# Eight of ten spectral blocks by seven half products of Strassen, transposed, with sixteen row scans moved behind them

## The chip, the cores and the metric

One Trainium2 chip, one core of it. The metric is the time in device microseconds of one execution of the whole kernel. The core has engines that run beside each other, each in the order of its own instructions: TensorE (PE in the profile, with PEld for its loads of weights), VectorE (DVE), ScalarE (ACT), GpSimd (POOL) and SyncE (SP), which here only issues transfers. An instruction that waits for a semaphore holds everything behind it on its engine. PSUM holds the results of matmuls, SBUF everything else on the core; DRAM is reached by DMA.

## What is computed

Everything is fp32; S = 2048 rows, D = 512 columns, 32 heads of 16.

```python
def reference(x, wqkv, wo, ..., dft_seq_re, dft_seq_im, dft_hid_re, dft_hid_im, gate_w):
    g = sigmoid((x * gate_w).sum(-1, keepdims=True))
    q, k, v = heads(x @ wqkv)                           # 32 heads of 16
    o = softmax(q @ k.T / 4) @ v                        # per head, 2048 x 2048 scores
    a = o @ wo
    re, im = x @ dft_hid_re.T, x @ dft_hid_im.T         # 2048 x 512
    y = dft_seq_re @ re - dft_seq_im @ im               # 2048 x 2048 by 2048 x 512, twice
    return g * a + (1 - g) * y
```

The part of the change is the second product of y, dft_seq_im times im. A "spectral block" t is 128 rows of it (128 x 2048 by 2048 x 512); there are sixteen.

## The kernel before, in words

**Numbers.** A product of two fp32 operands is made of three products of rounded parts: hi·hi, hi·lo, lo·hi, where hi is the operand rounded and lo is the rest. Each of them is issued as two matmuls of 64 rows (`halves_of`, L181), which run together into two PSUM banks. So a block of 128 x 128 times 128 x 512 is six matmuls, and a spectral block, with sixteen of these, 96.

**Front (to about 672 us).** The projections to q, k and v, re and im (im is kept negated, `b`; both are stored to DRAM in 128-row tiles, `ab_d`), the whole product with dft_seq_re, and the first six blocks with dft_seq_im. Beside these products run "scans". A scan (n of 0..1023, 64 for each of the 16 pairs of heads) gives the maximum of 512 scores for 128 rows, for two heads; the softmax needs the maxima of its pair before that pair's turn. `FRONT` = 724 scans are made in the front (660 of them folded: two matmuls L154, an ACT pass L158 for every other one, a DVE pass L160). How densely they stand beside the products is set by the spacings `PACE`, `SUMS`, `BESIDE`, `PART` and `SWAP`.

**Rear.** One loop over 512 "steps" (L1010): a pair p has 32 steps, step = 32p + i, with sixteen blocks of 128 keys for each half h of the queries. In a step the scores of one block of keys go to PSUM (`qk_both`, L234: one exp of 1024 columns; `qk_single`, L242: two of 512), and the exps of an earlier step are multiplied by the values (`pv`, L755). Beside that, a step has one more piece of work:

- steps 2 to 300: one scan (`next_scan`, L998: two matmuls L135, a DVE reduce L137), number n = 723 + step;
- from `MIX` = 301 on: one slot of `outputs()` (L961). First the ten spectral blocks t = 6..15, sixteen slots of six matmuls each (L907), to step 460; then, from `OUT` = 461, the product of the heads' outputs with wo (`mix_heads` for t = 0..15, then `mix_some`).

Scans and slots share one pair of PSUM banks (`pair_banks`, L743). On an odd step the order is scores, scores, slot; on an even one slot, scores, scores and two blocks of values' products.

**Buffers for the rows.** A pair's q and k rows (eight transfers, `row_loads`, L89 to L100, together 1.57 MB) live in two tiles of the pool `stk`, which has six: three pairs' worth. Who takes them: `load_use(p + 1)` at i = 18 of each pair, for the exps of the next pair (L1014; it also loads ones, L116, and the maxima `m_d`, L118); `load_scan`, for the next pair to be scanned, when n % 64 = 54 (L1002), ten scans before its first use; later `load_y` (L865), for y of four blocks at a time. The pair that is in use holds two tiles for its 32 steps, the pair that is scanned holds two for its 64 scans.

**Spectral operands.** For a spectral block the quarter blocks of dft_seq_im come from DRAM (`load_unit`, L883, tile `craw`, two buffers) and are split into hi and lo on DVE (L890, L891); im stays in SBUF in 32 tiles `b0` to `b31` (hi and lo). At the end of a block two DVE operations (L911) add it, times 1 − g, to the y of the front, which comes from and goes back to DRAM (`y_d`, L898 and L912). `load_y` fetches the sums at steps 436 (t = 0..7) and 480 (t = 8..15).

**Order of transfers.** All transfers named here are issued by SP, in the order of the program, and at most eight of them are under way: each waits for the end of the one eight places before it. The heads' outputs are written by POOL's queue (L774 `r_d`, L783 `o_d`). Near the end SP issues, in this order: the rows of the heads' outputs (`output_rows`, L847), then `output_last(1)` (L862), whose eight loads wait for the store `o_d` of the last pair but one, then the stores of the result (L945). `take_in` (L872) is the DVE operation that adds a finished product with wo, times g, to y.

Of the kernel before, what the change touches and what calls it, by code (L numbers as in the profile page):

```python
# [10 lines left out]
F32 = mybir.dt.float32  # L11
# [7 lines left out]
P = 128  # L19
# [27 lines left out]
MIX = TOTAL - FRONT + 1  # L47
OUT = MIX + NB * LATER
SLOW = 3
SCANS_IN = 0  # L50
AHEAD = (30, 31, 37, 44)


def build(tc, xT, wqkv, wo, wrT, wiT, cr, ci, gate, out):
    nc = tc.nc
    with ExitStack() as ctx:
# [12 lines left out]
        m_d = [dram.tile([2, 4, 2, NB, 32], F32, name=f"m_d{p}") for p in range(NP)]  # L69
        ab_d = [[dram.tile([P, D], F32, name=f"ab_d{i}_{t}") for t in range(NB)] for i in range(2)]  # L70
        y_d = [dram.tile([P, 4, D], F32, name=f"y_d{c}") for c in range(NC)]
# [115 lines left out]
        def block(i):  # L187
            return big.tile([P, 512], F32R, tag=f"b{i}", name=f"b{i}")
# [541 lines left out]
        with ExitStack() as pa:  # L730
# [12 lines left out]
            def pair_banks():  # L743
                return wide(SCANS_IN, "s1")
# [58 lines left out]
            def output_operands():  # L803

                for n in range(2 * ND - 2):
                    b = [block(6 + 2 * n + i) for i in range(2)]
                    raw = (ap.tile([P, D], F32, tag="craw", name="wor", bufs=2) if n == ND - 2 else
                           ap.tile([P, D], F32, tag="take", name="wor", bufs=3))
# [65 lines left out]

            raws, units = [], [(t, u) for t in range(NB - LATER, NB) for u in range(NU)]
            parts = []

            def load_unit():
                if units:
                    t, u = units.pop(0)  # L880
                    raw = ap.tile([P, D], F32, tag="craw", name="craw", bufs=2)
                    raws.append(raw.rearrange("p (c q) -> p c q", q=P))
                    nc.sync.dma_start(raws[-1], ci[t, :, u * CS:(u + 1) * CS, :])  # L883
# [30 lines left out]

            def take_in_beside(t, ps, add):

                o = ap.tile([P, D], F32, tag="take", name="take", bufs=2)
                nc.scalar.mul(o, ps, g[:, t:t + 1])
                add.tensor_add(ys[t], ys[t], o)

# [40 lines left out]
            def outputs():  # L961

                for t in range(NB - LATER, NB):
                    yield from spectral(t)
                for c in range(NC):
                    for t in range(4 * c, 4 * c + 4):
                        yield from mix_heads(t, (2, 2, 2, 3) if t < 2 * SLOW and t % 2 == 0 else (4, 5))
                    if c < 2:
                        output_rows(c + 2)
                for t in (8, 9, 10):  # L970
                    yield from mix_some(t, (0, 1))
                for t in range(3):
                    yield from mix_some(t, (0, 1))
                yield
# [35 lines left out]
            for step in range(NP * PERIODS):  # L1010
# [42 lines left out]
                if halved and halved[0][0] <= step:  # L1053
# [82 lines left out]
```

## Time and profile before

| | |
|---|---|
| time, median of 3 runs | 1726.67 us (1726.31 to 1727.58) |
| time of the profiled execution | 1727.06 us |
| its span in the profile | 1725.1 us |
| instructions | 36058 |
| bytes moved by DMA | 195.53 MB |
| L234, the exps of 1024 columns | 512 x 1131 ns |
| `craw<-ci` transfers | 64 of 256 KB |

The profile is that of one execution. Its page gives busy time for each engine (matmuls overlap, so PE's sum can be near the span while more work would fit), then the span in slices, the queues, a chain of what ended last, and groups of instructions. A group's line has its place in the code, engine, operation, output and inputs, the shape, the count, then busy time and mean, then the idle time ahead of it and what ended that. The view by windows gives, for a stretch of the span, each engine's busy time with its count of instructions, then TensorE's granted clock, the DMA engines' busy share and the GB/s moved. The timeline gives start, duration, engine, line, output and input; for SP an entry is the issue of a transfer, not its landing.

### The profile page before, as it was taken

The numbers are of one execution on the slowest core, as the hardware profiler recorded it, in microseconds if no ns is written. First come the engines' busy times: TensorE is split into PE (matmuls) and PEld (weight loads), VectorE is DVE, ScalarE is ACT, GpSimd is POOL, SyncE is SP. The second block draws the span as 40 slices with busy tenths as digits, with TensorE's granted clock in tenths as the row PEclk, the third lists the DMA queues.
The fourth block names the chain that finished last, engine by engine and source line by source line (L and its number), as shares of the span: only waits on it lengthen the run. The fifth ranks groups of instructions, "written<-read, shape, count | busy, mean of one in ns | idle before, by whom it ended". The sixth has DMA issues, their size and how long they took to land.

```text
span 1725.1 us, 36058 instructions
## 1 busy us (share of the span) xinstructions
PE 1711.2 (99%) x13656; PEld 1039.2 (60%) x13656; DVE 1089.1 (63%) x2060; ACT 1507.0 (87%) x2489; POOL 653.0 (38%) x774
## 2 busy tenths in 40 slices
PE   9999999999999999999999999999999999999998
PEld 6888888989888885333333333333455555555554
DVE  5898888999999996666666666666512222122333
ACT  6447889888888888999999999999988888888876
POOL 3672435655555762223223242322322322223222
PEclk9999999999999999999999999999999999999999
DMA  7783457533337763143323332251333254254723
GB/s 255 239 288 76 150 159 214 160 112 114 103 110 209 157 134 74 31 78 58 66 59 66 55 80 47 57 104 41 61 84 93 68 116 90 67 144 141 184 66 126
DMA packets 126750, 195.53 MB, mean 113 GB/s; under 512 B 56192, under 2 KB 58736, under 8 KB 119664
## 3 DMA queue, kind: packets, MB, share of 16 engines
q1 hardware_dynamic: 85392, 171.64, 37.4%
q0 software_dynamic: 40608, 20.54, 5.7%
q8 instruction: 107, 1.75, 0.4%
q10 hardware_dynamic: 576, 1.05, 0.2%
q14 instruction: 67, 0.55, 0.1%
HBM read 130.55 MB, written 63.18 MB: 112 GB/s over the span
## 4 chain that ended last, share of the span: by engine, by line
PE 95%; DMA 1%; DVE 1%; issue 1%; ACT 1%; POOL 0%; SPq 0%; DVEq 0%; POOLq 0%; ACTq 0%
PE pvb L755 28%; PE xy L185 25%; PE s L210 18%; PE s L154 10%; PE s L185 9%; PE s L135 5%; DMA q_d<-eh 0%; DMA raws<-wqkv 0%; DVE fold L160 0%; DMA b<-o_d 0%; PE s L554 0%; DVE y L872 0%; ACT fold L158 0%; DVE s L278 0%; DVE mx L137 0%
## 5 line engine op out<-in xcount | busy, mean ns | idle before, releaser
L234 ACT ACTIVATE eb<-s 128x1024 f32<-128x1024 f32 x512 | 578.9, 1131 | 64.5 <-PE s L210 64.4
L242 ACT ACTIVATE e<-s 128x512 f32<-128x512 f32 x1022 | 608.5, 707 | 0.4 <-PE s L210 0.4
L137 DVE TENSOR_REDUCE mx<-s 128x2 f32<-128x1024 f32 x364 | 441.3, 1224 | 188.6 <-PE s L135 188.2
L755 PE MATMUL pvb<-eb,va 128*17 128x512 f32 x2052 | 513.0, 597 | 0.0
L755 PE MATMUL pvb<-e,va 128*17 128x512 f32 x2044 | 512.1, 597 | 0.0
L160 DVE CUSTOM_DVE_ANT_0 fold<-s,fold 128x512 f32<-128x512 f32 x660 | 444.0, 690 | 52.5 <-PE s L154 24.3
L158 ACT ACTIVATE fold<-s 128x512 f32<-128x512 f32 x660 | 390.4, 604 | 72.8 <-PE s L154 50.5
L210 PEld LDWEIGHTS s<-qs,ks 50*128 50x128 f32 x2048 | 214.9, 184 | 355.4 <-ACT eb L234 254.9
L210 PE MATMUL s<-qs,ks 50*128 50x512 f32 x2048 | 420.4, 434 | 0.0
L185 PE MATMUL xy<-b,c 64*128 64x512 f32 x2448 | 396.9, 392 | 0.3 <-ACT c L333 0.3
L154 PE MATMUL s<-ks,qs 48*128 48x512 f32 x1320 | 314.4, 405 | 1.7 <-DVE mx L160 1.0
L185 PEld LDWEIGHTS xy<-b,c 64*128 64x128 f32 x2448 | 283.3, 187 | 17.0 <-issue 1.0
L154 PEld LDWEIGHTS s<-ks,qs 48*128 48x128 f32 x1320 | 172.7, 184 | 46.9 <-DVE mx L160 12.7
L774 POOL DMA_DIRECT2D r_d<-lc x31 | 18.2, 586 | 458.3 <-DVE lc L773 458.3
L755 PEld LDWEIGHTS pvb<-eb,va 128*17 128x17 f32 x2052 | 70.5, 96 | 189.8 <-issue 182.6
L135 PE MATMUL s<-ks,qs 48*128 48x512 f32 x728 | 151.7, 394 | 1.1 <-DVE mx L137 0.7
L767 POOL DMA_DIRECT2D lc<-ob x124 | 63.0, 515 | 155.0 <-DVE ob L764 154.7
L185 PE MATMUL xy<-w,b 64*128 64x512 f32 x768 | 115.2, 392 | 0.0
L365 POOL TENSOR_TENSOR c<-craw,c 128x512 fp32r<-128x512 f32 x84 | 109.6, 1304 | 6.7
L185 PE MATMUL s<-b,chi 64*128 64x512 f32 x654 | 103.0, 391 | 0.0
L364 POOL CAST c<-craw 128x512 fp32r<-128x512 f32 x84 | 53.4, 636 | 124.9 <-PE xy L185 119.9
L890 DVE CAST chi<-craw 128x512 fp32r<-128x512 f32 x40 | 19.7, 493 | 111.7 <-PE s L185 83.2
(133 smaller groups left out, 1532.2 us busy)
## 6 DMA issues: line engine op xcount, KB each, us to landing
qs<-q_d SPq DMA_DIRECT2D x66, 256.0 KB
craw<-ci SPq DMA_DIRECT2D x64, 256.0 KB
craw<-cr SPq DMA_DIRECT2D x60, 256.0 KB
ks<-k_d SPq DMA_DIRECT2D x44, 256.0 KB
qs<-q_d SPq DMA_DIRECT2D x66, 128.0 KB
ab_d<-ab SPq DMA_DIRECT2D x32, 256.0 KB
y_d<-y SPq DMA_DIRECT2D x32, 256.0 KB
o_d<-oh POOLq DMA_DIRECT2D x30, 256.0 KB, 13.3
```

The source lines that it names most:

```text
L135: nc.tensor.matmul(ps[:, j, :], qs[b:b + 48, qb * P:(qb + 1) * P], ks[b:b + 48, c * 512:(c + 1) * 512], start=True, stop=True)
L137: nc.vector.tensor_reduce(mx[p][:, :, qb, c], ps, axis=AX.X, op=ALU.max)
L154: nc.tensor.matmul(ps, qs[b:b + 48, qb * P:(qb + 1) * P], ks[b:b + 48, c * 512:(c + 1) * 512], start=True, stop=True)
L158: nc.scalar.activation(fold[j], ps, AF.Relu)
L160: nc.vector.tensor_tensor_reduce(out=fold[j], in0=ps, in1=fold[j], scale=1.0, scalar=-3.0e38, op0=ALU.add, op1=ALU.max, accum_out=mx[p][:, ...
L185: nc.tensor.matmul(ps[j], lhs[r], rhs[r], start=first, stop=last)
L210: nc.tensor.matmul(pss[j], ks[b:b + 50, kb * P:(kb + 1) * P], qs[b:b + 50, q0:q0 + 512], start=True, stop=True)
L234: nc.scalar.activation(e, ps, AF.Exp, scale=SCALE)
L242: nc.scalar.activation(e[j], pss[j], AF.Exp, scale=SCALE)
L365: sub(lo, raw, hi.bitcast(F32))
L755: nc.tensor.matmul(pvb[r:r + VC, :], va[:, kb, 2 * p + j, :], es[c][j], start=kb == 0, stop=kb == NB - 1, tile_position=(0, r))
L767: nc.gpsimd.dma_start(lc[32 * n:32 * n + 32, :], ob[r + DH:r + VC, :].rearrange("p (s e) -> p s e", e=16))
```

## The change

`FRONT` goes from 724 to 708: sixteen scans move from the front to the rear, whose `MIX` goes from 301 to 317 (`PART` from 2.07 to 2.15, so that the scans left are spread over the same products). Of the ten spectral blocks of the rear only t = 6 and 7 stay as they were (steps 317 to 348). The other eight, t = 8..15, are computed as one transposed product: 512 x 2048 (im transposed) by 2048 x 1024. It is cut into quadrants, 256 x 1024 by 1024 x 512, and in place of their eight products Strassen's seven are made (`CROSSES`: sums and differences of quadrants on the left and on the right), each in two halves f of 128 columns of im and eight slots: 112 slots of six matmuls in place of 128, steps 349 (`HALVED`) to 460. `OUT` stays 461.

For these products:

- twelve operands a product (`form_unit`): sums or differences of one or two 256 KB pieces, which `begin_unit` loads three steps ahead (the right operand from a new input `ct`, the left one from the stored im, in pieces of 128 columns); on DVE an addition or subtraction where there are two pieces, then a copy (hi) and a subtraction (lo). The tile `craw` has eight buffers in place of two;
- at the end of each half (`gather`) DVE copies one PSUM bank and adds the other, POOL adds it into the results that need it, and when a quadrant is done DVE transposes it in 32 x 32 squares (three steps later) and SP stores it to DRAM in four transfers (five to eleven steps later);
- at steps 482 to 489 the eight transposed blocks are loaded one by one (`load_turned`, tile with three buffers), and three steps later each is added to y on DVE (`take_turned`).

`output_rows(0)` moves from step 449 to 453. `load_y` for t = 8..15 stays at step 480. `take_in_beside`, which nothing calls, goes.

The core of the diff:

```diff
-FRONT = 564 + 16 * LATER
+CROSS = 8
+SAVED = 2 * CROSS
+FRONT = 564 + 16 * LATER - SAVED
-PACE, SUMS, BESIDE, PART, SWAP = 3.9, 5.2, 2.72, 2.07, 2.97
+PACE, SUMS, BESIDE, PART, SWAP = 3.9, 5.2, 2.72, 2.15, 2.97
 MIX = TOTAL - FRONT + 1
-OUT = MIX + NB * LATER
+OUT = MIX + NB * LATER - SAVED
+HALVED = MIX + NB * (LATER - CROSS)
+TURNED = 482
+CROSSES = [([((0, 0), 1), ((0, 1), 1)], [((1, 1), 1)]),
...
+            for n, (left, right) in enumerate(CROSSES):
+                crossed += [(NB * n + at, n, left if f is not None else right, f, u)
+                            for at, f, u in ((-8, 0, 0), (-6, None, 0), (-5, None, 1), (-4, None, 2), (-2, 0, 1),
+                                             (-1, None, 3), (0, None, 4), (2, None, 5), (3, None, 6), (4, None, 7),
+                                             (6, 1, 0), (7, 1, 1))]
+            def begin_unit(at, n, terms, f, u):
...
+                for (a, b), sign in terms:
+                    raw = ap.tile([P, 512], F32, tag="craw", name="craw", bufs=8)
+                    if f is None:
+                        nc.sync.dma_start(raw, ct[8 * a + u, :, 512 * b:512 * b + 512])
+                    else:
+                        e = 256 * a + P * f
+                        nc.sync.dma_start(raw.rearrange("p (s e) -> p s e", e=P),
+                                          b_d[2 * b + u][:, :, e:e + P].rearrange("s p e -> p s e"))
...
+            def form_unit(at, n, terms, f, u):
...
+                if len(raws) > 1:
+                    (nc.vector.tensor_add if terms[1][1] > 0 else nc.vector.tensor_sub)(raws[0], *raws)
...
+                nc.vector.tensor_copy(hi, raws[0])
+                nc.vector.tensor_sub(lo, raws[0], hi.bitcast(F32))
+            def finish(r, quadrant, f, x):
...
+                def square():
+                    turn.append(cw.tile([P, 512], F32, tag=("chi", "clo")[f], name="turn"))
+                    nc.vector.transpose(turn[0], x)
+                def store(a):
+                    e = 256 * k + P * f + 32 * a
+                    nc.sync.dma_start(yt_d[j].rearrange("(b i) e -> i b e", i=32)[:, :, e:e + 32],
+                                      turn[0][32 * a:32 * a + 32, :].rearrange("p (b e) -> p b e", e=32))
+                finishing.append((r + 3, square))
+                for a in range(4):
+                    finishing.append((r + 5 + 2 * a, lambda a=a: store(a)))
+            def gather(n, f, ps, r):
+                t = place(28 + f if n == 0 else 30 + f if n == 1 else None)
+                nc.vector.tensor_copy(t, ps[:, 0, :])
+                nc.vector.tensor_add(t, ps[:, 1, :], t)
...
+            def crosses():
+                for n in range(len(CROSSES)):
+                    for f in range(2):
+                        ps = pair_banks()
+                        for u in range(8):
+                            left, right = sets[f, u // CS], sets[None, u]
+                            q = slice((u % CS) * P, (u % CS + 1) * P)
+                            for i, (a, b) in enumerate(((0, 0), (0, 1), (1, 0))):
+                                halves_of((ps[:, 0, :], ps[:, 1, :]), left[a][:, q], right[b],
+                                          u == 0 and i == 0, u == 7 and i == 2)
+                            if u < 7:
+                                yield
+                        gather(n, f, ps, now[0] - HALVED)
+                        yield
+            def load_turned(t):
+                y = ap.tile([P, D], F32, tag="take", name="turned", bufs=3)
+                nc.sync.dma_start(y, yt_d[t // 4 - 2][(t % 4) * P:(t % 4 + 1) * P, :])
+                turned_[t] = y
+            def take_turned(t):
+                nc.vector.scalar_tensor_tensor(ys[t], turned_.pop(t), gm[:, t:t + 1], ys[t], op0=ALU.mult, op1=ALU.add)
...
-                for t in range(NB - LATER, NB):
+                for t in range(NB - LATER, NB - CROSS):
                     yield from spectral(t)
+                yield from crosses()
...
-                if step in (OUT - 12, OUT + 1):
+                if step in (OUT - 8, OUT + 1):
                     output_rows(int(step > OUT))
-                if step in (OUT - 25, (NP - 1) * PERIODS):
+                if step in (OUT - 25, TURNED - 2):
...
                 pend.append((p, h, kb, es))
+                crossing(step - HALVED)
+                if TURNED <= step < TURNED + CROSS:
+                    load_turned(NB - CROSS + step - TURNED)
+                if TURNED + 3 <= step < TURNED + 3 + CROSS:
+                    take_turned(NB - CROSS + step - TURNED - 3)
```

More of the change, by code (lines that the diff above doesn't have):

```diff
@@ L69, in build @@
         m_d = [dram.tile([2, 4, 2, NB, 32], F32, name=f"m_d{p}") for p in range(NP)]
-        ab_d = [[dram.tile([P, D], F32, name=f"ab_d{i}_{t}") for t in range(NB)] for i in range(2)]
+        b_d = [dram.tile([4, P, D], F32, name=f"b_d{n}") for n in range(NB // 4)]
+        ab_d = [[dram.tile([P, D], F32, name=f"ab_d_{t}") for t in range(NB)],
+                [b_d[t // 4][t % 4] for t in range(NB)]]
+        yt_d = [dram.tile([D, D], F32, name=f"yt_d{j}") for j in range(2)]
         y_d = [dram.tile([P, 4, D], F32, name=f"y_d{c}") for c in range(NC)]
@@ L913, in spectral @@
                 yield
[L915 to L919, printed above, removed]
+            crossed, begun, sets = [], {}, {}
+            for n, (left, right) in enumerate(CROSSES):
[3 more added lines that the diff above has]
+                                             (6, 1, 0), (7, 1, 1))]
@@ new lines, in form_unit @@
+            def form_unit(at, n, terms, f, u):
+                raws = begun.pop(at)
+                if len(raws) > 1:
+                    (nc.vector.tensor_add if terms[1][1] > 0 else nc.vector.tensor_sub)(raws[0], *raws)
+                base = 6 + 2 * u if f is None else 22 * f + 2 * u
+                hi, lo = block(base), block(base + 1)
+                nc.vector.tensor_copy(hi, raws[0])
+                nc.vector.tensor_sub(lo, raws[0], hi.bitcast(F32))
+                sets[f, u] = hi, lo
@@ new lines, in crossing, with place @@
+            def crossing(r):
+                for job in crossed:
+                    if job[0] == r + 3:
+                        begin_unit(*job)
+                for job in crossed:
+                    if job[0] == r:
+                        form_unit(*job)
+                for job in finishing[:]:
+                    if job[0] == r:
+                        finishing.remove(job)
+                        job[1]()
+            finishing, places, tiles = [], [0], {}
+            def place(i=None):
+                if i is None:
+                    i = (4, 5, 26, 27)[places[0] % 4]
+                    places[0] += 1
+                return block(i).bitcast(F32)
```

39 lines of the change are left out of this document (35 added, 4 removed), and 6 rows, old and new, of the table CROSSES.

## The prediction

> **What bounds the kernel now.** First the page: who is busy, and what the chain that ended last runs through.
>
> ```profile
> span 1725.1 us, 36058 instructions
> PE 1711.2 (99%) x13656; PEld 1039.2 (60%) x13656; DVE 1089.1 (63%) x2060; ACT 1507.0 (87%) x2489; POOL 653.0 (38%) x774
> PE 95%; DMA 1%; DVE 1%; issue 1%; ACT 1%; POOL 0%; SPq 0%; DVEq 0%; POOLq 0%; ACTq 0%
> ```
>
> TensorE's chain is the span. Which engine sets its pace differs by stage, so next the view by windows (busy time and count of PE, PEld, DVE, ACT, POOL; granted clock; DMA share; GB/s), for the front, the scan stage, the spectral stage and the stage of outputs:
>
> ```profile
> 400.00:425.00 25.00, 25.00 (x213) 22.58 (x213) 23.22 (x71) 22.06 (x40) 14.17 (x15) 1.00 0.35 101
> 700.00:1200.00 500.00, 500.00 (x3696) 191.42 (x3692) 338.79 (x312) 500.00 (x792) 151.02 (x227) 1.00 0.33 64
> 1238.00:1586.70 348.70, 348.70 (x2873) 184.86 (x2873) 71.44 (x126) 311.06 (x480) 95.69 (x143) 1.00 0.40 99
> 1588.00:1690.00 102.00, 102.00 (x830) 54.19 (x828) 34.12 (x51) 84.39 (x128) 28.38 (x43) 1.00 0.50 128
> ```
>
> The front is TensorE's: 25 us for 213 matmuls, 0.117 each. In the rear a step has three exps, so a step takes 500/264 = 1.894 us in the scan stage, where ACT is busy throughout, and 348.7/160 = 2.179 in the spectral stage, where ACT rests and TensorE sets the pace. No wait of TensorE is long anywhere: whatever the change makes TensorE wait for comes on top.
>
> **The change part by part.**
>
> *Work taken away.* Sixteen folded scans of two matmuls leave the front: 16 x 2 x 0.117 = 3.8 us. In the rear the number of steps stays, sixteen of them become scan steps in place of spectral ones: 16 x (2.179 - 1.894) = 4.6 us. The half products have the slots and matmuls of the blocks that they replace. Gain 8.4 us, where nothing is late.
>
> *Rows for the scans (the largest term).* `load_scan` is asked for when n % 64 = 54. That was step 35 + 64k and is now 51 + 64k, for pairs 12 to 15. Look at SyncE's timeline and waits:
>
> ```profile
> 672.75 0.58 SPq L100 DMA_DIRECT2D ks<-k_d  x1
> 676.64 0.56 SPq L100 DMA_DIRECT2D qs<-q_d  x1
> 725.23 0.56 SPq L100 DMA_DIRECT2D ks<-k_d  x1
> 730.84 0.60 SPq L100 DMA_DIRECT2D qs<-q_d  x1
> 757.19 0.56 SPq L100 DMA_DIRECT2D ks<-k_d  x1
> ...
> SPq L100 <- PE s L210: 224.0, 13, 46.1
> ```
>
> 725.23 is `load_scan(12)`: it waited for L210, the last use of pair 0 at step 31, and took its two tiles. 757.19 is `load_use(2)` at step 50; it took the tiles of pair 11, scanned until step 44. With the change step 50 comes first and takes pair 0's tiles; at step 51 the six tiles belong to the pair in use, the next one, and pair 11, whose last scan is now step 60. The built program says so: the first load of pair 12's rows waits for pair 11's last scan matmul, and pairs 13, 14 and 15 likewise. The scan of step 61 needs these rows. TensorE takes its instructions in order, so behind that scan stand step 61's other scores, the values' products and everything after. ACT then runs dry. Four times TensorE waits for eight loads, less one step.
>
> How long eight loads take is in the windows over two bursts of before:
>
> ```profile
> 672.00:674.00 2.00, 2.00 (x18) 0.67 (x14) 1.28 (x2) 1.95 (x4) 0.78 (x2) 1.00 0.35 131
> 674.00:676.00 2.00, 2.00 (x20) 0.72 (x22) 1.34 (x2) 2.00 (x4) 0.00 (x0) 1.00 0.94 229
> 682.00:684.00 2.00, 2.00 (x22) 0.67 (x14) 1.35 (x2) 2.00 (x4) 0.00 (x0) 1.00 0.64 53
> 735.00:737.00 2.00, 2.00 (x22) 0.70 (x14) 1.34 (x2) 2.00 (x4) 0.00 (x0) 1.00 1.04 143
> 737.00:739.00 2.00, 2.00 (x22) 0.72 (x14) 1.35 (x2) 2.00 (x5) 0.00 (x0) 1.00 0.27 45
> ...
> 726.20 0.88 POOL L783 DMA_DIRECT2D o_d<-oh  x1
> ```
>
> From 672.75 the DMA engines are full until about 683.2: 10.4 us, some small loads of maxima at its end. From 725.23 they are full until some 737.5: 12.3 us, beside the stores `o_d` that POOL began at 726.20. The bounds: 1.57 MB at the 229 GB/s of 674 to 676 and 0.6 for the issue, 7.5 us; and 12.3. The new bursts start three steps of 1.894 earlier in their pair than 725.23 did, so the first half runs ahead of those stores: I take 11. With 0.4 from the last scan to the first issue, less 1.9 of the step between: 9.5 us a stall (6.0 to 10.8), four times: **38 us** (24 to 43).
>
> By the Trainium skill ("DMA: Bandwidth & Descriptors", Specifications) HBM gives a core about 358 GB/s; by that estimate the same bytes take 4.4 us, the stalls some 20 us in all, and the sum would be 18 lower. The bursts here moved at most 229 GB/s in two microseconds, so the measurement decides.
>
> *Transposed blocks at the end.* Eight loads at steps 482 to 489, eight additions on DVE three steps later. SP, waits and timeline, and what they feed:
>
> ```profile
> SPq L862 <- DMA o_d<-oh: 20.6, 1, 20.6
> ...
> 1398.24 1.00 SPq L883 DMA_DIRECT2D craw<-ci  x2
> 1666.62 4.92 SPq L862 DMA_DIRECT2D b<-o_d  x8
> ...
> 1401.62 0.43 DVE L890 CAST chi<-craw 128x512 fp32r<-128x512 f32 x1 [7.89 <-DMA craw<-ci]
> 1662.11 1.54 DVE L872 SCALAR_TENSOR_TENSOR y<-s,g,y 128x512 f32<-128x512 f32 x2 [3.54 <-PE s L185]
> ...
> 1664.87 2.26 PE L185 MATMUL s<-b,b 64*128 64x512 f32 x18
> ```
>
> The loads of t = 13, 14 and 15 are issued behind `output_last(1)`, on whose store SP stood 20.6 us, to 1666.62, and whose eight loads took 4.92: 1671.5. A 256 KB load is there 3.4 us after its issue (1398.24 to 1401.62): 1674.9. On DVE the additions of 13 and 14 stand ahead of `take_in(12)`, at 1662.11 before: two at half of 1.54, so it is done at 1674.9 + 1.5 + 1.5 = 1677.9. It frees the banks that `mix_heads(13)` filled at 1664.87: TensorE stands **13 us** (10 to 16; the later loads run beside each other).
>
> *Clock.* Each of these five waits is an idle TensorE. The only long idle time in before is its end:
>
> ```profile
> 1717.00:1718.00 1.00, 0.63 (x6) 0.19 (x2) 1.00 (x3) 0.58 (x2) 0.92 (x1) 1.00 1.03 379
> 1722.00:1723.00 1.00, 0.00 (x0) 0.00 (x0) 0.00 (x0) 0.00 (x0) 0.00 (x0) 0.53 1.03 381
> ```
>
> After the last matmul, at 1717.6, the clock granted falls within 5 us to 0.53. So after each wait TensorE resumes at about half; no row shows for how long. From nothing lost to a whole step at half speed (1.9 us): I take the upper end, being certain that it starts slow, 2.0 x 5 = **10 us** (0 to 10).
>
> By the Trainium skill ("TensorE: Matmul & The Clock Gate", Part 1) the clock falls after an idle window of about 3.4 us and comes back after some 3.4 us of sustained work; the fall agrees with the row, and by that estimate it would be about 1.5 a stall, 2.5 less in all.
>
> *The half products' own stage.* DVE, which splits an operand in 0.49 + 0.69 and copies a bank in 0.69, and SP:
>
> ```profile
> L890 DVE CAST chi<-craw 128x512 fp32r<-128x512 f32 x40 | 19.7, 493 | 111.7 <-PE s L185 83.2 <-DMA craw<-ci 19.8 <-DMA qs<-q_d 8.7
> L891 DVE TENSOR_TENSOR clo<-craw,chi 128x512 fp32r<-128x512 f32 x40 | 27.7, 692 | 2.7
> L764 DVE COPY ob<-pvb 128x512 f32<-128x512 f32 x31 | 21.4, 692 | 85.7 <-PE pvb L755 84.2
> ...
> 1378.61 0.69 SPq L100 DMA_DIRECT2D ks<-k_d  x1
> ...
> 1518.58 0.58 SPq L100 DMA_DIRECT2D ks<-k_d  x1
> 1537.07 1.24 SPq L867 DMA_DIRECT2D y<-y_d  x2
> 1538.40 1.17 SPq L883 DMA_DIRECT2D craw<-ci  x2
> ```
>
> In sixteen steps (35 us) DVE gets twelve operands of up to 0.69 + 0.49 + 0.69 and two gathers of 1.4: about 26 us, where there were some 5. It fits, though each slot's operand now hangs on one wait further up. Before each second product stand `load_use`'s loads on SP, 19.6 us at 1378.61 to 1398.24, 18.5 at 1518.58 to 1537.07, there with two 1 MB loads of y behind. The operands of the product then come through one queue, about 21 loads of 256 KB each 35 us. SP runs up to eight buffers ahead of the steps, which covers most of such a hold; the one with the loads of y is about 7 us too long by this count, another about 1. Bounds: nothing (all covered), and 20 (each of four holds late by 5). I take **6**.
>
> *The rest.* The transposes (0.7 each, eight) and the stores of quadrants fall on DVE and SP with time to spare; POOL gains some twenty additions on an engine 38% busy; the end of a half frees its banks after two DVE operations, 1.4 us, while a step's scores and values' products (about 3 us) run: no cost. If that cover failed it would be up to 1.4 x 14 = 20, held in the stage's bound.
>
> **The sum**, against the profiled execution's 1727.06 (span 1725.1 and 2.0 around it; 0.4 above the median of 1726.67): -3.8 - 4.6 + 38 + 13 + 10 + 6 = +58.6, span 1783.7, time 1785.7; say **1786**.
>
> **Rivals.**
>
> *The half products' operands are late throughout.* Each of 84 operands hangs on SP's order. If each `load_use` in the stage, and the stores of quadrants on the same queue, cost 10 us in place of 6 in all, 4 x 10 - 6 = +34: 1820. For it: 18 to 20 us holds in the rows above. Against: eight buffers, loads asked three steps ahead.
>
> *No stall for rows.* If the rows' tiles came free otherwise, the four stalls and their clock (38 + 8) fall away: 1740. Against: the built program's waits.
>
> *Faster.* One mechanism: every new load lands under work queued ahead of it, TensorE never stands. That needs the rows within one step, 1.9 us after the last scan, and the transposed block 13 by 1662; the price is then zero, and the 8.4 us of work are the whole: 1719. It decides at 1.9 us; the bursts above took 10.
>
> *The change saves nothing and costs nothing.* A stage limited by ACT would swallow the saved matmuls; the front and the step times above speak against it, and it would need the waits to vanish too.
>
> **How the numbers follow.** Forecast 0.73 (1786), late operands 0.13 (1820), no row stalls 0.08 (1740), faster 0.05 (1719), no difference 0.01. Low end: -8.4 + 24 + 10 + 0 + 0 = +25.6, 1753; high end of the forecast's own: -8.4 + 43 + 16 + 10 + 20 = +81, 1808. To reach into the late-operand case: 1750 to 1820. A difference of 0.2% (3.5 us) is about what a measurement of this kernel can tell from none: faster 0.05, same 0.01, slower 0.94.
>
> **What would show it.** Right: four idle stretches of TensorE of some 9 us in the scan stage, 121 us apart, ended by the DMA `ks<-k_d` or `qs<-q_d` ahead of L149 (before's L135), ACT idle with it; a granted clock under 1.00 behind each; one idle stretch of some 13 us at about step 493, ended by DVE's `take_in`, with DVE waiting for `turned<-yt_d`; SP waiting there for `o_d<-oh`; spectral-stage steps near 2.18 but for single gaps at operands. Wrong: a scan stage without gaps (the sum then falls by 46), gaps under 6 or above 11 us (the rate of the bursts misjudged), a clock that stays at 1.00, or steps of the half products that are slower all through, with TensorE waiting for DVE.

## The result and the profile after

The changed kernel takes 1818.94 us (median of 4 runs, 1815.75 to 1819.48) against 1726.49 for the kernel before: a ratio of 1.0532 (95% interval 1.0513 to 1.0550), +92 us. The forecast was 1786, its range 1750 to 1820. The lines of the code have moved by 14 (L135 is L149, L210 is L224, L185 is L199).

The page of the changed kernel, the lines that answer to those shown of before, with the row of the granted clock in 40 slices:

```profile
span 1814.0 us, 36252 instructions
PE 1726.3 (95%) x13560; PEld 1036.5 (57%) x13560; DVE 1221.7 (67%) x2236; ACT 1498.6 (83%) x2473; POOL 675.9 (37%) x790
PEclk9999999999999999989989989989999999989989
...
PE 84%; DMA 8%; DVE 2%; SPq 2%; POOL 2%; issue 1%; ACT 0%; DVEq 0%; POOLq 0%
...
L149 PE MATMUL s<-ks,qs 48*128 48x512 f32 x760 | 162.5, 400 | 42.3 <-DMA qs<-q_d 41.6
```

TensorE's share falls from 99% to 95%, the chain now runs through DMA for 8%, and in the scan stage the clock dips four times at equal distances. To see where the time came in, take the copies of the bank `pvb` that DVE makes after each half of a pair, every sixteen steps (L764 before, L778 after, 31 times), as mileposts. (A copy that stands on DVE behind other work is late as a milepost though TensorE may lose nothing; such a part comes back at the next one.) Here are two of the changed kernel's timeline (before they are at 758.60 and 789.01):

```profile
752.91 0.69 DVE L778 COPY ob<-pvb 128x512 f32<-128x512 f32 x1
...
796.22 0.69 DVE L778 COPY ob<-pvb 128x512 f32<-128x512 f32 x1
```

Sixteen scan steps took 30.41 before and 43.31 now: 12.9 lost between steps 48 and 64. All 31 mileposts, each kernel's profiled execution less that of before, grouped by stage (stage of the half products: steps 320 to 480; end: 480 to 496):

| us against before | front | four row waits | cheaper steps | half products | end | median |
|---|---|---|---|---|---|---|
| forecast | -3.8 | 46 | -4.6 | 6 | 15 | 1786 |
| changed kernel | -5.6 | 55.5 | -4.8 | 28.1 | 17.0 | 1818.9 |
| scans_only | -6.4 | 56.0 | -4.8 | 0.0 | 0.4 | 1769.4 |
| phase_kept | -0.6 | -0.1 | 0.0 | 25.2 | 18.0 | 1768.6 |
| turned_early | -6.3 | 56.6 | -4.8 | 35.8 | 0.1 | 1799.4 |
| adds_dve | -3.4 | 56.9 | -4.8 | 27.7 | 17.5 | 1814.0 |
| spread | -5.6 | 54.5 | -4.8 | 20.9 | 18.1 | 1811.5 |
| divide_late | -5.7 | 55.2 | -4.8 | 24.9 | 16.9 | 1813.2 |
| spread_late | -6.4 | 55.9 | -4.8 | 25.8 | 17.3 | 1811.7 |
| late_y | -6.5 | 55.6 | -4.8 | 20.0 | 20.1 | 1809.6 |
| late_y_spread | -6.6 | 55.4 | -4.8 | 15.2 | 16.7 | 1804.1 |
| all_fixed | -1.2 | -0.1 | 0.0 | 1.3 | 0.0 | 1728.4 |
| best | -4.2 | 0.7 | -4.8 | 12.1 | 0.0 | 1729.8 |
| best3 | -6.0 | 0.3 | -4.8 | 10.4 | 0.0 | 1728.7 |

(In the forecast's row each wait's clock, 2.0, is added to its wait. all_fixed and phase_kept have sixteen emptier steps inside "half products".) Each row is one execution. The front moved by up to 3 us between executions of the same front, and the times of one changed kernel spread by 3 to 14 us, widest in adds_dve (1806 to 1820); a few us between two rows inside the half products may be chance.

**A wait for rows.** The first of the four in the changed kernel's timeline of SP, and all four in TensorE's:

```profile
774.35 0.56 SPq L114 DMA_DIRECT2D ks<-k_d  x1
...
778.19 0.42 SPq L114 DMA_DIRECT2D qs<-q_d  x1
```

```profile
781.95 0.76 PE L149 MATMUL s<-ks,qs 48*128 48x512 f32 x1 [5.97 <-DMA qs<-q_d]
786.54 0.76 PE L149 MATMUL s<-ks,qs 48*128 48x512 f32 x1 [3.83 <-DMA qs<-q_d]
...
916.80 0.76 PE L149 MATMUL s<-ks,qs 48*128 48x512 f32 x1 [6.68 <-DMA qs<-q_d]
921.77 0.76 PE L149 MATMUL s<-ks,qs 48*128 48x512 f32 x1 [4.20 <-DMA qs<-q_d]
...
1053.09 0.76 PE L149 MATMUL s<-ks,qs 48*128 48x512 f32 x1 [7.11 <-DMA qs<-q_d]
1057.88 0.76 PE L149 MATMUL s<-ks,qs 48*128 48x512 f32 x1 [4.04 <-DMA qs<-q_d]
...
1188.45 0.76 PE L149 MATMUL s<-ks,qs 48*128 48x512 f32 x1 [6.19 <-DMA qs<-q_d]
1192.80 0.76 PE L149 MATMUL s<-ks,qs 48*128 48x512 f32 x1 [3.58 <-DMA qs<-q_d]
```

All eight loads are issued within 4.3 us. In the first wait TensorE stands 5.97 for the first head's rows, does one matmul of the scan, and stands 3.83 for the second's: 9.8 idle; 10.9, 11.2 and 9.8 in the others. The windows over the first show what comes on top:

```profile
784.00:785.00 1.00, 0.00 (x0) 0.00 (x0) 0.00 (x0) 0.00 (x0) 1.00 (x2) 0.50 0.19 16
786.00:787.00 1.00, 0.46 (x2) 0.49 (x3) 0.00 (x0) 0.00 (x0) 0.35 (x1) 0.50 0.33 32
790.00:791.00 1.00, 1.00 (x6) 0.33 (x2) 0.24 (x1) 0.67 (x1) 0.00 (x0) 0.50 0.27 70
791.00:792.00 1.00, 1.00 (x10) 0.15 (x8) 1.00 (x2) 1.00 (x3) 0.00 (x0) 0.76 0.23 86
```

The DMA engines are all but still from 784.2, TensorE goes on at 786.5, and its clock stays at 0.50 until 791.5: 4.9 us at half speed. 12.9 lost less 9.8 idle leaves 3.1; half speed over 4.9 us makes 2.5 of it, and the single scan matmul between the two stands, 0.76 at half speed, some 0.4.

**The end.** DVE, SP and TensorE of the changed kernel, three timelines:

```profile
1748.79 1.44 DVE L1053 SCALAR_TENSOR_TENSOR y<-turned,gm,y 128x512 f32<-128x512 f32 x2 [17.64 <-DMA turned<-yt_d]
1750.15 1.53 DVE L886 SCALAR_TENSOR_TENSOR y<-s,g,y 128x512 f32<-128x512 f32 x2
...
1740.82 4.92 SPq L876 DMA_DIRECT2D b<-o_d  x8
1745.84 1.48 SPq L1049 DMA_DIRECT2D turned<-yt_d  x3
...
1751.73 4.21 PE L199 MATMUL s<-b,b 64*128 64x512 f32 x18 [14.12 <-DVE y L886]
```

The loads of t = 13 to 15 are issued behind `output_last(1)`; two additions and `take_in(12)` wait for them, and TensorE for that, 14.1 us.

**The stage of the half products.** It lost 28 us, at three places (steps 368 to 384: 5.5; 400 to 416: 11.1; 432 to 448: 13.3). First what TensorE itself waited for there, one line at the first place, two at the second, one at the third:

```profile
1472.02 1.04 PE L769 MATMUL pvb<-eb,va 128*17 128x512 f32 x2 [3.81 <-DVE ob L778]
...
1540.40 2.93 PE L199 MATMUL s<-b,b 64*128 64x512 f32 x12 [6.35 <-DVE b L1005]
1554.00 0.61 PE L769 MATMUL pvb<-eb,va 128*17 128x512 f32 x2 [0.25 <-DVE ob L778]
...
1622.00 2.93 PE L199 MATMUL s<-b,b 64*128 64x512 f32 x12 [8.19 <-DVE b L1005]
```

L1005 is the second DVE operation of `gather`, which frees the banks of a half. The second place in the timelines of SP, DVE and POOL:

```profile
1505.71 1.29 SPq L114 DMA_DIRECT2D ks<-k_d  x1
...
1523.42 0.95 SPq L946 DMA_DIRECT2D craw<-b_d  x2
```

```profile
1527.22 0.69 DVE L955 TENSOR_TENSOR craw<-craw 128x512 f32<-128x512 f32 x1 [8.23 <-DMA craw<-b_d]
...
1536.95 0.25 DVE L787 RECIPROCAL lc<-lc 128x16 f32<-128x16 f32 x1
...
1539.65 0.69 DVE L1005 TENSOR_TENSOR b<-s,b 128x512 f32<-128x512 f32 x1
...
1552.66 0.71 DVE L990 STREAM_TRANSPOSE turn<-b 128x512 f32<-128x512 f32 x1 [6.95 <-POOL b L1018]
1553.30 0.65 DVE L778 COPY ob<-pvb 128x512 f32<-128x512 f32 x1
```

```profile
1537.49 0.57 POOL L788 DMA_DIRECT2D r_d<-lc  x1 [19.05 <-DVE lc L787]
1541.20 2.09 POOL L790 DMA_DIRECT2D rb<-r_d  x4 [3.13 <-DMA r_d<-lc]
1546.36 1.28 POOL L791 TENSOR_TENSOR ob<-ob,rb 128x512 f32<-128x512 f32 x1 [3.07 <-DMA rb<-r_d]
...
1549.61 0.88 POOL L797 DMA_DIRECT2D o_d<-oh  x1
...
1551.32 1.30 POOL L1018 TENSOR_TENSOR b<-b,b 128x512 f32<-128x512 f32 x1
```

Read from the top: SP issues an operand's load only at 1523.42, behind the loads of `load_use` that began at 1505.71. DVE stands 8.23 us for it, and what is behind it on DVE is late: the reciprocal and the gather, for which TensorE waits 6.35. That wait and the slow clock after it are this place's loss. A second queue forms at the same time: POOL's division has waited 19.05 us for the reciprocal, and then for its own two transfers; the gather's addition (L1018) stands behind all of it, although POOL is busy only 37% of the span; DVE's transpose waits for the addition, and `pvb`'s copy behind the transpose. Here TensorE waits only 0.25 us for that copy; at the first place the same chain (there DVE's transpose waited 10.28 us for POOL, again after DVE had stood 7.38 us for an operand) costs it 3.81. The late copy is also the milepost: 1.3 of the 11.1 us come back by step 432, and 1.4 of the 13.3 at the third place by 464. So the three places lose 6.4, 9.8 and 11.9, the first behind POOL, the other two behind late operands.

Were the operands late because the DMA engines were full? Two windows, in each of which DVE stands for an operand, at the second place and the third:

```profile
1520.00:1525.00 5.00, 5.00 (x44) 2.70 (x42) 0.00 (x0) 4.16 (x7) 0.00 (x0) 1.00 0.22 54
1610.00:1615.00 5.00, 3.80 (x32) 1.53 (x28) 2.49 (x5) 4.53 (x8) 0.00 (x0) 1.00 1.05 366
```

At the second place the engines were 0.22 busy: there the order on SP held the load. At the third, behind the two 1 MB loads of y, they were full.

### The profile page after: what moved, and what is told of

It reads as the page before. It is cut to its first block, busy times and chain, and to the rows that moved or that the text cites. A ratio compares the mean times of both kernels' runs of the same rounds, so it can differ in the third digit from the quotient of the medians.

```text
span 1814.0 us, 36252 instructions
## 1 busy us (share of the span) xinstructions
PE 1726.3 (95%) x13560; PEld 1036.5 (57%) x13560; DVE 1221.7 (67%) x2236; ACT 1498.6 (83%) x2473; POOL 675.9 (37%) x790
## 2 busy tenths in 40 slices
DMA packets 177057, 224.91 MB, mean 124 GB/s; under 512 B 74753, under 2 KB 101873, under 8 KB 169969
## 4 chain that ended last, share of the span: by engine, by line
PE 84%; DMA 8%; DVE 2%; SPq 2%; POOL 2%; issue 1%; ACT 0%; DVEq 0%; POOLq 0%
PE xy L199 25%; PE pvb L769 23%; PE s L224 15%; PE s L168 9%; PE s L199 6%; PE s L149 5%; DMA qs<-q_d 4%; SPq L114 1%; DMA craw<-b_d 1%; DMA rb<-r_d 1%; DMA craw<-ct 1%; DMA r_d<-lc 1%; DMA o_d<-oh 1%; DVE craw L955 0%; POOL rb L790 0%
## 5 line engine op out<-in xcount | busy, mean ns | idle before, releaser
L151 DVE TENSOR_REDUCE mx<-s 128x2 f32<-128x1024 f32 x380 | 460.9, 1224 | 253.7 <-PE s L149 205.4
L769 PE MATMUL pvb<-eb,va 128*17 128x512 f32 x2052 | 523.7, 606 | 4.4 <-DVE ob L778 4.4
L769 PE MATMUL pvb<-e,va 128*17 128x512 f32 x2044 | 522.8, 606 | 0.0
L174 DVE CUSTOM_DVE_ANT_0 fold<-s,fold 128x512 f32<-128x512 f32 x644 | 433.0, 690 | 57.6 <-PE s L168 29.8
L172 ACT ACTIVATE fold<-s 128x512 f32<-128x512 f32 x644 | 381.2, 603 | 77.5 <-PE s L168 59.1
L224 PE MATMUL s<-qs,ks 50*128 50x512 f32 x2048 | 429.7, 441 | 0.0
L224 PEld LDWEIGHTS s<-qs,ks 50*128 50x128 f32 x2048 | 216.8, 187 | 368.7 <-ACT eb L248 261.9
L199 PE MATMUL xy<-b,c 64*128 64x512 f32 x2448 | 394.5, 392 | 0.2 <-ACT c L347 0.2
L199 PEld LDWEIGHTS xy<-b,c 64*128 64x128 f32 x2448 | 284.7, 187 | 18.4 <-issue 1.0
L149 PE MATMUL s<-ks,qs 48*128 48x512 f32 x760 | 162.5, 400 | 42.3 <-DMA qs<-q_d 41.6
L168 PEld LDWEIGHTS s<-ks,qs 48*128 48x128 f32 x1288 | 166.9, 184 | 41.1 <-DVE mx L174 11.1
L199 PE MATMUL s<-b,b 64*128 64x512 f32 x1050 | 142.5, 403 | 29.0 <-DVE b L1005 14.5
L199 PEld LDWEIGHTS s<-b,b 64*128 64x128 f32 x1050 | 103.1, 191 | 55.6 <-DVE b L1005 15.4
L199 PE MATMUL xy<-w,b 64*128 64x512 f32 x768 | 114.6, 392 | 0.0
L149 PEld LDWEIGHTS s<-ks,qs 48*128 48x128 f32 x760 | 77.8, 186 | 49.5 <-issue 40.7
```

The lines of the kernel that those rows point to most:

```text
L149: nc.tensor.matmul(ps[:, j, :], qs[b:b + 48, qb * P:(qb + 1) * P], ks[b:b + 48, c * 512:(c + 1) * 512], start=True, stop=True)
L151: nc.vector.tensor_reduce(mx[p][:, :, qb, c], ps, axis=AX.X, op=ALU.max)
L168: nc.tensor.matmul(ps, qs[b:b + 48, qb * P:(qb + 1) * P], ks[b:b + 48, c * 512:(c + 1) * 512], start=True, stop=True)
L172: nc.scalar.activation(fold[j], ps, AF.Relu)
L174: nc.vector.tensor_tensor_reduce(out=fold[j], in0=ps, in1=fold[j], scale=1.0, scalar=-3.0e38, op0=ALU.add, op1=ALU.max, accum_out=mx[p][:, ...
L199: nc.tensor.matmul(ps[j], lhs[r], rhs[r], start=first, stop=last)
```

## The experiments

Own theory: three causes, each a queue in order. The rows' loads find no free tiles; the transposed blocks stand on SP behind `output_last(1)`; in the stage of the half products POOL's additions stand behind the division and operands on SP behind `load_use`. Rival for the whole: the change moves 224.91 MB in place of 195.53, and its transfers are late because the DMA engines are full.

**scans_only** (kernel before; `PART` goes to 2.15 too. It leaves out block 15's product with dft_seq_im, so its output lacks that part)

```diff
-FRONT = 564 + 16 * LATER
+FRONT = 564 + 16 * LATER - 16
...
-OUT = MIX + NB * LATER
+OUT = MIX + NB * (LATER - 1)
...
-                for t in range(NB - LATER, NB):
+                for t in range(NB - LATER, NB - 1):
                     yield from spectral(t)
```

> The kernel before with FRONT 708 alone: sixteen scans moved to the rear (MIX 317), spectral blocks as before, but block 15's product with dft_seq_im is left out so that OUT stays 461. Own theory (the last scan of pairs 11 to 14 now comes ten steps after load_use has taken the free tiles, so load_scan waits for it): four stalls of 12.8 to 15.0 us as in the changed kernel, 55.4 in all, with -5.6 in the front and -4.8 for the cheaper steps: 1726.5 + 45 = 1771.5. Rival (the rows are slow because the changed kernel moves 29 MB more): no such transfer runs here in that stage, so no stall beyond the step: 1716.

Measured: 1769.39 (ratio 1.0248, 1.0227 to 1.0268). The four waits are there, 56.0 us, with no transfer of the half products in the kernel. Its waits of TensorE:

```profile
PE s L135 <- DMA qs<-q_d: 42.2, 8, 7.0
```

Eight waits, two for each of the four, as in the changed kernel (41.6). Moving sixteen scans alone costs what it does there. The rival is out for this term.

**phase_kept** (changed kernel; `PART` goes back to 2.07 too)

```diff
-FRONT = 564 + 16 * LATER - SAVED
+FRONT = 564 + 16 * LATER
...
-OUT = MIX + NB * LATER - SAVED
+OUT = MIX + NB * LATER
...
                 yield from crosses()
+                for _ in range(SAVED):
+                    yield
```

> The changed kernel with FRONT back at 724 and sixteen empty slots ahead of OUT. Own theory: scans end at step 44 + 64k again, load_scan finds free tiles, the four stalls (55.4) go; the front's 5.6 comes back; empty steps cost about what scan steps do. The stage of the half products meets load_use at another product (three times instead of four, and no load of y beside it), so its 28 us become 15 to 28; the wait at the end (17) stays: 1755 to 1769. Rival (extra traffic makes the rows late): stalls in the scan stage stay in part, over 1785.

Measured: 1768.58 (1.0240, 1.0224 to 1.0255). No wait for rows is left; the other two losses stay:

```profile
PE s L199 <- DVE y L886: 16.1, 1, 16.1
PE s L199 <- DVE b L1005: 12.9, 3, 7.6
```

The two runs take the change apart: scans alone +43, half products alone +42, together 85 of the 92. Not expected: the empty slots are steps 445 to 460, and from milepost 448 to 464 the sixteen steps took 34.8 us, 2.18 each, no less than steps with six matmuls. The values' products are made in twos on even steps there, and neither TensorE nor ACT is full in a window amid them (23.58 and 24.59 of 28):

```profile
1590.00:1618.00 28.00, 23.58 (x170) 8.98 (x168) 3.34 (x7) 24.59 (x38) 7.33 (x10) 1.00 0.69 181
```

So the saved matmuls bring nothing by themselves.

**turned_early** (changed kernel)

```diff
-                y = ap.tile([P, D], F32, tag="take", name="turned", bufs=3)
+                y = ap.tile([P, D], F32, tag="craw", name="turned", bufs=8)
...
-                if TURNED <= step < TURNED + CROSS:
+                if TURNED - 9 <= step < TURNED - 9 + CROSS:
...
```

> The changed kernel with the eight loads of transposed blocks asked at steps 473 to 480 into the tile craw (eight buffers, free by then), ahead of output_last(1) on SP; the additions stay where they are. Own theory (the loads stand behind eight loads that wait for o_d): TensorE's wait of 14.1 at take_in and the slow clock after it go, 17 us: 1802. Rival (the blocks are late because the transposed stores are, in pieces of 128 bytes): the additions still wait, 1812 or more.

Measured: 1799.39 (1.0415, 1.0398 to 1.0433), 19.6 under the changed kernel. The end loses 0.1 in place of 17.0. The theory holds. Its profiled execution was its slowest, 1807, and the stage of the half products lost 35.8 in it where the changed kernel's lost 28.1: that stage seems to vary by several us from execution to execution.

**adds_dve** (changed kernel)

```diff
-                add, sub = nc.gpsimd.tensor_add, nc.gpsimd.tensor_sub
+                add, sub = nc.vector.tensor_add, nc.vector.tensor_sub
```

> The changed kernel with the gathers' twenty additions on DVE instead of POOL. Own theory (the additions stand on POOL behind the division's chain r_d, rb, o_d, and DVE's transposes wait for them, 10.3, 7.0 and 7.2 us, with the copy of pvb behind): these three waits go, some 5 us of TensorE each: 1802 to 1808. Rival (DVE is the bound of the stage): twenty operations of 0.7 more on DVE make operands later: 1819 or more.

Measured: 1813.99 (1.0504, 1.0474 to 1.0533), between the two expectations. The loss at steps 320 to 400 falls from 6.4 to 1.8; those at 400 to 448 don't (23.0 before, 25.9 now). The waits for POOL go, and TensorE waits for the gather instead, which stands on DVE behind late operands: 22.0 us in three waits, where it was 14.5 in two.

**spread** (changed kernel; `loads` are the fourteen transfers of `load_use`)

```diff
+                if p > 10:
+                    trickle.extend(loads)
...
+                for _ in range(min(len(trickle), 2 if i > 22 else 1)):
+                    trickle.pop(0)()
```

> The changed kernel with the fourteen transfers of load_use (from pair 11's on) asked one or two a step over steps i = 18 to 27 instead of all at i = 18. Own theory (operand loads stand on SP behind them): TensorE's waits for the gather behind late operands, 6.4 and 8.2 us and the slow clock after them, about 18 of the stage's 28 us, go; those by POOL stay: 1798 to 1806. Rival (the DMA engines, busy 0.9 there, are the limit, so order changes nothing): 1812 or more.

Measured: 1811.49 (1.0497, 1.0480 to 1.0513). About 7 us under the changed kernel, where 18 were expected; that is half a us from the rival's 1812. The stage loses 20.9 in place of 28.1. At steps 400 to 416 it is 6.3 in place of 11.1; at 432 to 448, where two loads of y stand as well, nothing is gained (14.7 against 13.3).

**divide_late** (changed kernel)

```diff
-                    halved.append((step + (10 if done[0] < NP - 2 else 7 if done[0] < NP - 1 else 3), quotients(*done[:2])))
+                    halved.append((step + (10 + 4 * (HALVED <= step < OUT - 16) if done[0] < NP - 2 else 7 if done[0] < NP - 1 else 3), quotients(*done[:2])))
```

> The changed kernel with the division of a half's outputs asked four steps later in the stage of the half products, behind the gather's additions on POOL, which else are as they were. Own theory (DVE's transposes wait for additions that stand on POOL behind the division's DMAs): the 6.4 at step 384 goes, and the share of POOL in the two other losses, some 5 each, too: 1802 to 1812. Rival (as in the run with the additions on DVE, the time is only waited elsewhere, for operands): 1813 or more.

Measured: 1813.17 (1.0506, 1.0491 to 1.0520), the rival's time. At steps 320 to 416 the stage loses 1.9 in place of 17.5, more than TensorE waited behind POOL there: with the division out of the way the operands come in time too, SP issuing the first load behind `load_use` 9.0 us after the copy of step 400 in place of 16.2. How moving the division does this stays open. But 15.7 are lost at steps 416 to 448 (11.9 in the changed kernel), and 7.4 appear at 448 to 480, for which this edit leaves the division where it was and the last transpose waits:

```profile
DVE turn L990 <- POOL b L1028: 12.9, 1, 12.9
```

**spread_late** (both)

> Both of these edits. Own theory: the two causes are all that the stage of the half products loses, 28 us: of them 6 or less are left, 1790 to 1797. Rival (rate of the DMA engines): 1808 or more.

Measured: 1811.67 (1.0479, 1.0455 to 1.0503). Missed by 15, and in the range of the rival: 0.8 left to step 416, but 14.6 at 416 to 448 and 10.4 after it. The two edits together do nothing for the loss at 416 to 448.

**late_y** (division late up to OUT, and)

```diff
-                if step in (OUT - 25, TURNED - 2):
+                if step in (OUT - 11, TURNED - 2):
```

> The changed kernel with the division four steps later up to OUT (the last run with it stopped sixteen steps before, and 7 us came back at steps 448 to 480 in a transpose that waited 12.9 us for POOL) and the two 1 MB loads of y for t = 0 to 7 at step 450, behind the last operand load, instead of 436. Own theory: the 14 us that stay at steps 432 to 448 are operands that stand on SP behind load_use and these two loads; without the latter they fall to 5 or less: 28 us of the stage become 5 to 9, 1797 to 1802. Rival (the hold by load_use alone is enough there): 1805 or more.

Measured: 1809.58 (1.0475, 1.0459 to 1.0491). Missed: 11.4 are left at 416 to 448, where divide_late had 15.7, so the hold by `load_use` is nearly enough there, as the rival said.

**late_y_spread** (late_y with spread)

> The same with load_use's transfers one or two a step. Own theory: what is left of SP's hold goes, the stage loses 4 or less: 1791 to 1796. Rival (what is left is the rate of the DMA engines or DVE): as the kernel without the spreading, within 3 us.

Measured: 1804.14 (1.0449, 1.0434 to 1.0463). The expectation missed by 8. 6.1 left at 416 to 448: beside a late division, moving y's loads alone gains 4.3 there, spreading `load_use` alone 1.1, both 9.6, so both held operands and either was nearly enough. At 448 to 480, 7.7: the last division, now at step 464, delays the transfer `lc` of the next half, and DVE's reciprocal waits for that ahead of `take_in`:

```profile
DVE lc L791 <- DMA lc<-ob: 13.4, 2, 9.8
```

**all_fixed** (spread, divide_late, turned_early and phase_kept, and)

```diff
-                for _ in range(min(len(pend), 1) if step < MIX else 0 if step % 2 else 2):
+                for _ in range(min(len(pend), 1) if step < MIX else 1 if OUT - SAVED <= step < OUT else 0 if step % 2 else 2):
```

> Both of these edits, the early loads of the transposed blocks and FRONT 724 with sixteen empty slots, in which the values' products are made one block a step instead of two every other step (in the empty slots of the earlier run a step took 2.18 us although TensorE and ACT both waited). Own theory: of that run's 1768.6 go 18 at the end, 24.5 in the stage of the half products and 4.6 in the empty steps: 1722, at 1718 to 1732. Rival (rate of the DMA engines in that stage): 1740 or more.

Measured: 1728.42 (1.0011, 1.0002 to 1.0020). As expected. With all causes treated at once, and the scans back in the front, the time is within 0.2% of before, though the same 224.9 MB are moved, so the rival's 1740 is out: 5.6 us are lost up to step 432, and 4.6 gained from 432 to 464, where one block of values a step makes the empty steps shorter (31.8 us from 448 to 464).

**best** (changed kernel with late_y_spread and turned_early, and the rows of pairs 12 and 14 in `craw`)

```diff
+            if p < NP and p % 2 == 0:
+                qs, ks = ([apart[0].tile([P, 512], F32R, tag="craw", name=name, bufs=8) for c in range(4)]
+                          for name in ("qs", "ks"))
...
-                if n % SCANS == SCANS - 10:
+                if n % SCANS == SCANS - 28:
```

> The changed kernel with the division later, y later, load_use spread, the transposed blocks early, and the rows of pairs 12 and 14 loaded into the eight craw tiles, which are idle in the scan stage, by load_scan 28 scans ahead instead of 10 (so FRONT stays 708). Own theory: none of the four waits for rows, nor the one at the end; -5.6 and -4.8 stay, the stage of the half products loses up to 5: 1716 to 1721, the only kernel here under the kernel before. Rival (the front's and the steps' gain is given back in the stage of the half products): 1726 or more.

Measured: 1729.81 (1.0023, 1.0014 to 1.0032). The four waits are gone with the scans still in the rear, once the rows of pairs 12 and 14 have tiles of their own and all rows are asked for 18 scans earlier (the run doesn't separate the two); the front's and the steps' gain, about 9, is there at step 400. It is given back in the half products (12.1), as the rival said:

```profile
PE s L222 <- DVE b L1029: 5.4, 3, 2.7
PE s L222 <- DVE y L910: 2.9, 1, 2.9
```

**best3** (best with `load_use` from i = 2 on, one transfer every other step; division late up to step 444; the last addition on DVE)

> The run named best with three edits at what its trace still shows: load_use (from pair 11's on) asked at i = 2 and issued one transfer every other step; the division later only up to step 444 (the one at step 464 delayed the transfer lc of the next half, and DVE's reciprocal waited 7.9 us for it ahead of take_in: 4.3 us at steps 464 to 480); the last half's addition on DVE, so that its transpose doesn't wait for POOL. Own theory: the 4.3 goes and of the 7.8 at steps 416 to 448 (operands beside load_use, DMA engines full) at least half: 1719 to 1724, under the kernel before. Rival (the stage is at the rate of the DMA engines, whatever the order): the 7.8 stays, 1725 or more.

Measured: 1728.72 (1.0008, 0.9999 to 1.0017). At the two places it was aimed at it gained 3.4 (416 to 448) and lost 0.2 (448 to 480: the loss at 464 to 480 went, and 4.2 came at 448 to 464); TensorE still waits 5.9 in three waits for gathers. The expectation missed by five, and the time is in the rival's range; whether what is left is the DMA engines' rate or the order on DVE wasn't settled. The windows of best3 over most of the stage:

```profile
1300.00:1560.00 260.00, 256.84 (x2096) 133.93 (x2092) 183.97 (x272) 226.94 (x350) 84.92 (x107) 0.99 0.74 194
```

The DMA engines are 0.74 busy and DVE 0.71, where in before these were 0.41 and 0.20 in the same window; such means can't tell which of the two decides at a given wait.

## Why the prediction was right, and where not

- *Right in kind:* all five waits predicted are where the forecast put them and wait for what it named. scans_only and phase_kept show the four row waits, turned_early the one at the end, each by taking it away alone.
- *Work taken away:* -5.6 and -4.8 against -3.8 and -4.6.
- *Rows:* 9.8 to 11.2 us idle a wait against 9.5, the third just over the 11 that was named as a sign of a wrong rate. The landing, taken as 11, was 12.2 from first issue to TensorE's start (of which work left over covered 1.6 and the scan's first matmul 0.8): the bytes were in after about 10, and TensorE saw them 2.3 later, which the bursts' rows of DMA busy time could not show.
- *Clock:* taken as 2.0 a wait, called the upper end; it was 3.0 to 3.9 (12.9, 14.7, 15.0 and 12.8 lost, less 9.8, 10.9, 11.2 and 9.8 idle). The bound was wrong: half speed lasts 4.9 us after the first wait, 6.2 and 6.7 after the second and third, not the 3.8 that a step of 1.9 us takes at half speed.
- *The end:* 14.1 idle and 3 of clock, 17.0, against 13 and 2.
- *The failed step is "The half products' own stage", with "The rest":* 6 taken, 0 to 20 as bounds, 28.1 measured. Three terms in it were mis-sized. The end of a half was taken as free, since its two DVE operations last 1.4 us; but they stand on DVE behind the operands, and TensorE waited 6.35 and 8.19 us for them, 9.8 and 11.9 lost with the clock. The hold of operands by `load_use` and y behind this was real but costed at 1 and 7: with both out of the way, 6.1 of divide_late's 15.7 are left at steps 416 to 448 (late_y_spread). POOL's additions were costed at nothing because POOL was 38% busy: the wait that they made at step 384 lost 6.4, and divide_late, which only moves the division behind them, takes away 15.6 of 17.5 us up to step 416. What the last 6 are, rate or order, stays open.
- *The rival "operands late throughout"* gave 1820, almost the measured time, but by another sum: it had 40 us in that stage. It was half right, since two of the three places wait for late operands. The time near the range's upper end is rows +9, half products +22, end +2. The forecast's own high end was 1808; only the margin for this rival reached 1820, so it is partly luck that the time lies under that.
- *Slips in the working:* "121 us apart" leaves out the waits themselves; they came 135 apart (781.95 to 916.80). The estimate of some 20 us of stalls beside the rows leaves out what the sum takes off for the step between; by the sum's own terms it would be 4.4 + 0.6 + 0.4 - 1.9, four times: 14. In the estimate beside the clock, 3.4 us at half speed lose 1.7 a stall, not 1.5.

## What to carry to other kernels

A busy share says nothing about what an instruction costs behind others: before new work goes on an engine "with time to spare", list the waits queued ahead of it there and who waits for its result. An operation is as late as what stands ahead of it in its queue, however short it is. When the phase of a loop moves, look at what else shares its buffers by the step at which each is asked for and freed, not at the count alone. A wait of TensorE of 6 us or more cost its length and, here, three to four us more; and a stage in which several queues are short of slack gives its loss back at the next place when only one is relieved.

## What the runs showed that was not expected

After waits of 10 to 14 us TensorE's granted clock stayed at 0.50 for 4.9 us (786.5 to 791.5), 6.2 (921.8 to 928.0), 6.7 (1057.9 to 1064.6) and 5.7 (1751.7 to 1757.5) of work, after the first three waits for rows and the wait at the end. Windows of the changed kernel around the last three returns:

```profile
927.00:928.00 1.00, 1.00 (x8) 0.00 (x0) 0.30 (x2) 0.56 (x2) 0.00 (x0) 0.50 0.26 70
928.00:929.00 1.00, 1.00 (x10) 0.49 (x6) 0.12 (x1) 0.35 (x1) 0.00 (x0) 0.99 0.26 68
...
1064.00:1065.00 1.00, 1.00 (x10) 0.61 (x6) 0.00 (x0) 0.08 (x1) 0.00 (x0) 0.72 0.32 100
...
1756.00:1757.00 1.00, 1.00 (x8) 0.23 (x10) 0.96 (x2) 0.59 (x1) 0.00 (x0) 0.50 0.00 0
1757.00:1758.00 1.00, 1.00 (x12) 0.16 (x8) 0.52 (x1) 1.00 (x3) 0.00 (x0) 0.77 0.00 0
```

The Trainium skill ("TensorE: Matmul & The Clock Gate", Part 1) gives one busy window of about 3.4 us before full clock, and calls the window free-running, with a variation of half a us; these four lie 1.5 to 3.3 us above 3.4, and the measurement decides. An estimate that fits them, from the page's window: a full window that begins after the work does would end 3.4 to 6.8 us after it. The forecast used the shorter figure beside its sum.

A transfer's end was seen by TensorE 2.3 us after the DMA engines fell still (784.2 to 786.5). The Trainium skill ("DMA: Bandwidth & Descriptors", Anatomy of one DMA) gives a transfer on GpSimd's path a fixed cost of about 2 us, most of it the confirmation that the last byte has landed; the 2.3 us here, on SP's queue, are near that.

Steps with nothing beside them were no cheaper than steps with six matmuls (2.18 us), as long as the values' products came in twos; in ones (all_fixed) the same sixteen took 1.99 each.
